# A block-recurrent attention with an activated two-layer product: 69 elementwise steps moved to GpSimd, fewer filler products, new orders

## The chip, the core and the metric

The kernel runs on one core of a Trainium2 chip. A core has five engines with a queue each: TensorE (PE, matrix products from SBUF into PSUM), VectorE (DVE), ScalarE (ACT, activations and copies), GpSimd (POOL) and SyncE (SP, which issues transfers). ACT and POOL can issue transfers as well. Each engine works off its own instructions in the order in which they were written, and waits on semaphores for the others. The metric is the device time of one execution in microseconds. Times are medians of a few runs; the profile is of one more execution.

## The reference

All data are float32. Attention part, with `x` of 8 x 8 x 512 x 64 and `state` of 8 x 8 x 32 x 64:

```python
scores = scale * x @ state^T ;  a = softmax(scores) ;  xread = a @ state
scores2 = scale * state @ x^T ; a2 = softmax(scores2) ; sread = a2 @ x
attn = concatenate([xread, sread], axis=2)          # 8 x 8 x 544 x 64
```

Then, on the 4352 rows of 512 that this gives:

```python
h = rows @ w_in                                     # 512 -> 2048
g = h * erf(softplus(h))
out = g @ w_out                                     # 2048 -> 512
```

## The kernel before

**Tiling.** A batch `b` (eight of them) has 512 token rows and 32 state rows. Batch 0 is computed plainly while the weights arrive. For the others the hidden width is cut in two halves `u`: a first phase does batches 1 to 7 with half 0 (`unit(b, 0, ...)`), then the state rows of all batches are done, then a second phase does batches 1 to 7 and 0 with half 1. The products use a scheme with seven block products instead of eight (`seven`, `second_product`), in the second phase and for the last two batches of the first one twice over (`twice_product`). Such a scheme trades matmuls for sums of blocks. Those sums are much of VectorE's work:

- `mixed` (L838 to L854): the state of a batch times a half of `w_in`, evicted by ACT into `m`, and four sums of 128x512 (L849).
- `sums_y` (L875): four sums of 128x256 of the transposed attention weights, per batch.
- `first_product` (L937): seven products give `h` through PSUM; ACT copies (L949), DVE adds (L951, L955), ACT takes Softplus (L959).
- `serf` (L974, L977): Erf on ACT, then the product with `h` on DVE; `sums_a` (L988): four sums of 128x1024 on DVE.
- `twice_product` (L1239 sums of the left factor, L1257 products, L1267 copies, L1272 adds). `total` (L1182) adds two results before they are stored. `put` stores over POOL's queue with an add into memory (L1177) or over SP's queue (L1174). In the last batch `join_others` reads back what is stored, adds the rest (`join`, L1189) and stores (`store`, L1193); the last stores are at L1306.

**Conversion of the weights.** The weights arrive as 64-bit numbers in `raw`. `convert` makes float32 of them in five steps: ACT scales the upper words (L558) and the lower words (L560), DVE shifts (L562), adds the lower part (L564) and puts the sign in (L566). The first eight pieces are converted in the prologue; for the second half of the weights, `stage` fetches and converts sixteen smaller pieces during the first phase.

**The prologue.** `begin0` computes batch 0's scores, softmax and transposes. Between its steps PE runs filler products (`spare_products`, which calls `warm`, L115): products of the identity with itself, whose results nobody reads. Each is two records of 128x128.

**The order of the work.** Nothing is issued where it stands in the code. Every step is entered by `op(engine, cost, at, go, reads, writes, ...)`, which notes on which earlier steps it depends. `ORDER` holds for each engine a list written out by hand in which order its steps stand in its queue. `emit` walks these lists with the given costs to find a common order of starts, and writes the instructions in it. The costs decide nothing on an engine: there the list alone counts. `either` (L152 to L175) puts a copy on DVE if its name is in the set `BY_VECTOR`, and on ACT otherwise.

**What is where.** GpSimd computes nothing but the identity at the start; its queue holds transfers: the fetches of the second half of the weights (L543, L549), stores of converted weights and the accumulating stores (L1177).

Of the kernel before, what the change touches and what calls it, by code (L numbers as in the profile page):

```python
# [9 lines left out]
F32 = mybir.dt.float32  # L10
# [7 lines left out]
def kernel(  # L18
# [121 lines left out]
    def op(engine, cost, at, go, reads=(), writes=(), table=None, land=0.0, pipe=0.0):  # L140
# [14 lines left out]
        x1 st s01 ta0 ta1 z1 m020 m021 u0 u1 m120 m121 sn11 sn40 sn41 sn51 sn70""".split())  # L155

    def either(name, cost, out, in_, at, reads, writes, by=None):

        def vector():
            if by:  # L160
                nc.vector.tensor_scalar(out(), in_(), by(), None, op0=ALU.mult)
            else:
                nc.vector.tensor_copy(out(), in_())

        def scalar():
            if by:
                nc.scalar.activation(out=out(), in_=in_(), func=ACTF.Copy, scale=by())
            else:
                nc.scalar.copy(out(), in_())

        if name in BY_VECTOR:
            op(DVE, cost[1], at, vector, reads, writes)
        else:
            op(ACT, cost[0], at, scalar, reads, writes)
# [3 lines left out]
            0 5 1-2 8 3 6 4 9 15 7 10 12 22 13 16-18 25 19-20 11 23-24 14 26 28 27 29-30 21 32 31  # L178
            33-34 70 54 69 53 61 45-46 62 55 35 64 36-37 47 38 72 40 39 50 41 58 57 71 73 63 49 43
            52 42 48 60 56 44 77-78 59 79 51 76 82 81 83 80 66 84-85 93 86-87 75 68 89 74 88 90 65  # L180
            67 92 91 102 106 94 97 107 103-104 108 105 109 118 95 110-111 114-115 112 96 113 116
            98-99 117 130 119 122 132-133 123 131 134 124-125 137 135 120 136 140 139 138 141 121
            142-143 100 144 126 101 127-129 145 147 149-151 177 153-154 179-180 155 178 181 184 165
            182 166 152 167 183 161 187 168 156 186 185 188 157-158 189 159 190 162-164 191 146 160
            148 169-170 192 194 171-172 224 196-197 173-174 198-199 226 225 227 175 200 176 228 231
            201-202 212 203 229 208 230 204-205 233 206 234 232 209 235 210 213 236 211 237 207 214
            216 238 193 217-219 195 215 241 239 220-221 243-245 271 246 222 273 240 223 274 247
            251-252 272 275 242 255 276 248 278 256 277 249 281 257 280 279 250 259 282 253 260 284
            283 254 258 285-286 261 263-265 288 287 266 318 262 290 321 291 267 322 292 319 289 268
            323 293 269-270 320 298 294 325 295 324 296 299 327-328 302 300 303 329 301 304 326 305  # L190
            330 297 331 310-312 306 313 307-309 333 332 334 364 314-315 336 366 316 365 367 317 337
            339 368 343 338 371 344 369 345 370 347 335 373 340 374 341-342 346 375 372 349 406 376
            348 350 377 357 407 351 408 359 358 353 360 352 361 354 410 355 363 362 356 385 409 387
            386 388 378 389 411 390-391 379-382 412-413 383 399 384 414-415 392 401 416 418-419 417
            394 434 393 435 395-396 403 438 400 402 404 440 397 441 436 398 405 437 442-443 439
            444-446 432 422-423 447 428 424-425 449 448 430 433 464 420-421 429 426 467 466 427 431
            468 465 471 469-470 450 474 473 472 475 451 462 476-477 454-455 452-453 479 478 456
            458-459 508 457 460 463 461 511 509 487 510 480 489 488 512 515 481 490 513 491 483 482
            492 518 484 514 519 493 517 516 520 501 485-486 521 494 522-523 495-496 502 552 503-504
            497-498 553 505 555 554 506-507 556 499 531 500 532-533 524 558 535 557 534 559 536-537  # L200
            526 525 560 528 562 545 561 563 529 527 564-565 530 547 567 566 549 546 538 548 596 540
            539 598 541-542 599 551 600 603 550 543 575 544 576-578 597 579 568 602 601 580 569-570
            606 572 604 607 605 581 571 608-609 573 610-611 574 589 640 590-592 582 642 593 643 583
            594 644 647 595 584 619 641 586 585 620 645 587-588 621 646 612 650 613 615 614 623 622
            648 651 616 624 652 618 617 653 626 649 625 655 654 628 627 633 630 684 629 634 636 687
            685-686 635 688 637 689 638 632 690 639 691 631 693 663 694 656 664 695 692 665 657 659
            667 666 658 697 668 696 660 699 698 669 661 728 677 662 678-679 731 670 729-730 681 672
            680 671 674 673 675-676 682 732 700 683 701 733 707 734 709 708 735 711 702 710 703-704
            712 738 736 706 705 737 739 714 713 740-741 721 715 722-723 716-717 725 742-743 726 718
            724 719 772 727 774-775 720 773 751 776 744 777 746 779 752 745 753 747 782 781 778 755  # L210
            754 783 748 780 784 756-757 749 785 765 750 766 758 768 767 759-762 769 763-764 770 786
            771 787-790 793 791 795 794 792 797 800 796 801-802 798-799 804 803 807 805-806 808-809
            814 810-811 816 815 812 817-818 813 819-820""",
        ACT: """
            0-3 5 10 4 11-12 6-7 13 8-9 30 29 14 31 15-17 52 32 53 19 18 33-37 20-21 38 22-23 39-40
            25 24 41-43 28 26-27 45 48 44 47 46 50 54-55 49 51 56 61 64 63 62 65 57-58 67 66 68 70
            69 71-72 92 91 73-74 83 101 76 102 84-85 75 77 60 86 79-80 78 81-82 87-89 131 90 99 132
            59 96 100 143 97 93 103-104 94-95 98 133 135 134 145 136 144 147 107 149 106 108 148 138
            105 139 150 137 146 151 156 153 158 157 155 159 154 162 160-161 152 141 140 163-165 142
            169-170 166-167 176 175 113 172 168 171 185-187 111 188 178-179 181 189 194 109-110 112  # L220
            196 177 114 191 197-198 193 195 192 190 199-200 208 183 174 173 207 201 180 202-203 182
            210-211 184 204 117 209 205 212 120 221 119 206 223 115 222 118 224 214 116 217 215 225
            230-232 213 235 233 226 228 234 236 219 227 237 218 123 229 238 124 243 239 244 220 216
            240-241 126 249 121 125 248 245-246 242 122 258 247 130 259 129 254 260-261 251 250 262
            267 252-253 265 269-270 268 263 266 264 127 271-274 128 280 255-256 283 282 275 281 276
            286 277 285 287 284 296 278 257 298-299 279 292 300 297 289 288 305 290 306 302 307 310
            301 291 303 308-309 294 311 304 312-316 295 317 321 318 320 319 344 293 345 322 324 346
            329 347-348 330 325 353 351 332 327 323 349 326 355 331 354 328 350 358 356 359 334 352
            357 360 333 339 361-362 340 363-365 335 386 341 336 342 337 343 371 338 372 374 373
            366-367 369 368 375 370 387-388 381 389 376 390-391 382 377-378 392 399 393 384 394-396  # L230
            379 397-398 383 385 380 401-402 405 407 403 406 400 415 414 412-413 404 408-409 417
            410-411 418-419 422 420 423 421 426 428 427 429 425 432 424 431 430 433-437 440 439 441
            416 442 463 438 465 448 443 464 466 449 451 467 472 444 452 474 445-446 450 475 471 458
            468 473 447 469 476 470 479 477 453 478 485 487 480 488 481-482 454 486 483 459 484 509
            461 511 460 456 455 512 457 462 494-495 510 489 496-497 513 498 514 490 517-518 492 520
            519 521 504 491 523-524 522 516 515 525-526 505 527-528 533 507 531 493 499 534 532 555
            529 500 506 501 530 556-557 502 508 540-541 503 558 543 535 544 559 564 542 536 566 563
            567 561-562 565 538 570 537 568 560 571 539 572 579 578 577 580 550 569 601 551 573-574
            545 553 603 552 602 575-576 554 586 546 604 548 547 605 610 587 549 581 607 582 612 589
# [589 lines left out]
    def mixed(b, u, at):  # L829
# [17 lines left out]
        def sub(o, x, y, how=ALU.subtract):  # L847
            v = views_x()
            tt(v[o - 1], v[x - 1], v[y - 1], op=how)  # L849
# [20 lines left out]
    def sums_y(b, at):  # L870
        y_of = Y_of(b)

        def sub(o, x, y):
            v = views_a(b)
            tt(v[o - 1], v[x - 1], v[y - 1], op=ALU.subtract)  # L875
# [839 lines left out]
```

## Time and profile before

| | us |
|---|---|
| median of 3 runs | 698.82 (698.72 to 699.63) |
| the profiled execution | 699.4 |
| its span, first to last instruction | 697.6 |
| PE busy | 690.2 (99%) |
| DVE busy | 586.3 (84%) |
| ACT busy | 467.3 (67%) |
| POOL busy | 85.9 (12%) |
| PE's last matmul ends | 693.15 |
| dense products start (L614) | 20.71 |

The clock granted to TensorE is 1.00 over the run. HBM traffic averages 132 GB/s. A line of the groups shows the code line, the engine, the operation, output<-input, shapes and count, then busy time, the mean of one in ns, the idle time of the engine before them and what ended it. `PEq`, `SPq` and `POOLq` are what an engine's sequencer does by itself. Matmul ends in the trace are modelled, so PE's stalls are better read from the view of waits than from its busy time.

### The profile page before, as it was taken

The page shows a single profiled execution, that of the slowest core. Times are in us where ns is not written, and L with a number is a line of the kernel's source. Part 1 is how long each engine was busy: PE and PEld are TensorE (multiplying, and loading weights), DVE is VectorE, ACT ScalarE, POOL GpSimd, SP SyncE. Part 2 cuts the span into 40 slices and gives each one's busy share as a digit, 9 for nine tenths or more (in the row PEclk, how much of TensorE's full clock was granted, in tenths as well). Part 3 has the DMA queues.
Part 4 walks back from the last instruction along what each step waited for, and adds up shares of the span by engine and source line. Part 5 has one row for each costly group of instructions (what it writes and reads, how often), then busy time and mean ns, then how long its engine had stood idle before and what let it go on. Part 6 is the DMA issues. An engine that isn't in the chain of part 4 may idle for free.

```text
span 697.6 us, 13137 instructions
## 1 busy us (share of the span) xinstructions
PE 690.2 (99%) x5193; PEld 583.9 (84%) x5193; DVE 586.3 (84%) x900; ACT 467.3 (67%) x847; POOL 85.9 (12%) x93
## 2 busy tenths in 40 slices
PE   9999999999999999999999999999999999999997
PEld 8534678787878888899998879898989898998996
DVE  5999899998989999988945679696959696869797
ACT  5987988869596766756263774858485748385832
POOL 0000110102010010000200200002322133022332
PEclk9999999999999999999999999999999999999999
DMA  8858878867968854140729311213736158026495
GB/s 263 231 144 170 216 177 212 221 143 238 239 210 180 230 166 181 62 167 1 160 83 346 47 54 46 69 16 80 95 73 87 55 65 155 1 31 92 64 148 106
DMA packets 133741, 92.87 MB, mean 133 GB/s; under 512 B 93744, under 2 KB 120752, under 8 KB 133168
## 3 DMA queue, kind: packets, MB, share of 16 engines
q1 hardware_dynamic: 114336, 61.88, 32.0%
q0 software_dynamic: 18800, 29.63, 22.5%
q8 instruction: 41, 0.67, 0.4%
q10 hardware_dynamic: 544, 0.52, 0.2%
q14 instruction: 20, 0.16, 0.1%
HBM read 50.86 MB, written 41.16 MB: 132 GB/s over the span
## 4 chain that ended last, share of the span: by engine, by line
PE 89%; DVE 4%; ACT 1%; issue 0%; DVEq 0%
PE o L1257 29%; PE h L937 19%; PE o L1021 18%; PE at L937 7%; PE o L1440 4%; PE o L639 2%; PE h L1391 2%; PE at L838 2%; PE h L838 2%; PE at L799 1%; PE h L706 1%; PE at L1391 1%; DVE ring L977 1%; PE at L614 1%; DVE ring L988 0%
## 5 line engine op out<-in xcount | busy, mean ns | idle before, releaser
L949 ACT COPY ring<-h 128x512 f32<-128x512 f32 x120 | 69.8, 586 | 70.2 <-PE h L937 63.8
L977 DVE TENSOR_TENSOR ring<-ring 128x1024 f32<-128x1024 f32 (+1 forms) x64 | 73.3, 1153 | 23.9 <-ACT ring L974 23.9
L937 PE MATMUL h<-aT,m 128*128 128x256 f32 x360 | 91.6, 381 | 0.2 <-ACT m L844 0.2
L1021 PE MATMUL o<-w_out,ring 128*128 128x256 f32 x320 | 77.7, 382 | 0.0
L959 ACT ACTIVATE ring<-ring 128x512 f32<-128x512 f32 x120 | 72.5, 634 | 6.5 <-PE o L1257 3.7
L937 PEld LDWEIGHTS h<-aT,m 128*128 128x128 f32 x360 | 65.5, 190 | 10.1 <-issue 1.3
L988 DVE TENSOR_TENSOR ring<-ring 128x1024 f32<-128x1024 f32 x60 | 72.8, 1218 | 0.4
L1021 PEld LDWEIGHTS o<-w_out,ring 128*128 128x128 f32 x320 | 59.6, 190 | 11.9 <-DVE m L566 1.7
L1257 PE MATMUL o<-w_out,w_in 128*128 128x128 f32 x512 | 69.1, 276 | 0.3 <-DVE ring L1282 0.3
L1257 PEld LDWEIGHTS o<-w_out,w_in 128*128 128x128 f32 x512 | 64.7, 192 | 2.8 <-issue 0.8
L1257 PE MATMUL o<-w_out,ring 128*128 128x128 f32 x480 | 64.8, 276 | 0.1
L974 ACT ACTIVATE ring<-ring 128x1024 f32<-128x1024 f32 (+1 forms) x64 | 62.4, 1005 | 0.2
L1257 PEld LDWEIGHTS o<-w_out,ring 128*128 128x128 f32 x480 | 60.4, 192 | 1.8 <-DVE ot L1272 0.3
L1021 PE MATMUL o<-raw,ring 128*128 128x256 f32 x240 | 59.8, 380 | 0.0
L1021 PEld LDWEIGHTS o<-raw,ring 128*128 128x128 f32 x240 | 45.2, 190 | 8.6 <-issue 2.5
L1257 PE MATMUL o<-raw,ring 128*128 128x128 f32 x360 | 49.6, 276 | 0.1
L1257 PEld LDWEIGHTS o<-raw,ring 128*128 128x128 f32 x360 | 46.1, 192 | 2.1 <-ACT ring L974 0.8
L1177 POOL DMA_DIRECT2D out_dram<-oo x16 | 25.9, 1736 | 164.5 <-DVE m L1239 77.8
L1257 PE MATMUL o<-raw,xT 128*128 128x128 f32 x320 | 41.8, 277 | 0.0
L1257 PEld LDWEIGHTS o<-raw,xT 128*128 128x128 f32 x320 | 38.6, 192 | 2.4 <-ACT ring L959 0.8
L1177 POOL DMA_DIRECT2D out_dram<-m x15 | 22.1, 1624 | 104.9 <-ACT ring L959 38.2
L937 PE MATMUL h<-sy,sx 128*128 128x256 f32 x120 | 31.2, 382 | 0.0
(269 smaller groups left out, 1400.5 us busy)
## 6 DMA issues: line engine op xcount, KB each, us to landing
x<-in_x_dram SPq DMA_DIRECT2D x30, 256.0 KB, 4.7
xq<-in_x_dram SPq DMA_DIRECT2D x112, 64.0 KB, 2.5
out_dram<-oo SPq DMA_DIRECT2D x10, 512.0 KB, 3.6
raw<-in_moe_w_in_dram SPq DMA_DIRECT2D x8, 512.0 KB, 6.6
raw<-in_moe_w_out_dram SPq DMA_DIRECT2D x4, 1024.0 KB, 7.4
kept_a<-aT SPq DMA_DIRECT2D x8, 512.0 KB, 4.8
raw<-in_moe_w_out_dram POOLq DMA_DIRECT2D x8, 512.0 KB, 5.7
raw<-in_moe_w_in_dram POOLq DMA_DIRECT2D x8, 512.0 KB, 5.7
```

The source lines that it names most:

```text
L838: nc.tensor.matmul(out=bank(names[k])[Ns * p:Ns * p + Ns, :], lhsT=st[r, b, q], rhs=of_group[2 * u + j][r, :, i, :], start=True, stop=True)
L937: nc.tensor.matmul(out=out_[:, i], lhsT=x_[:, q:q + P], rhs=y_, start=(start and i == 0), stop=(i == 1), skip_group_check=not start)
L949: op(ACT, 0.5, t, lambda: nc.scalar.copy(out_(), view(bank(name))), [name], w)
L959: op(ACT, 0.53, t, lambda: nc.scalar.activation(out=part(splane, k), in_=part(hplane, k), func=ACTF.Softplus), area(hplane, ks=[k], os=[o] ...
L974: op(ACT, 0.085 + 0.875 * share, at + n, lambda s_=s_: nc.scalar.activation(out=s_, in_=s_, func=ACTF.Erf), [], area(splane, ks=[k], os=os ...
L977: op(DVE, 0.065 + 1.075 * share, at + n + 1, lambda s_=s_, h_=h_: tt(s_, s_, h_, op=ALU.mult), area(hplane, ks=[k], os=os), area(splane, k ...
L988: op(DVE, 1.14, at + k, lambda k=k, x_=x_, y_=y_, how=how: tt(get("h", k), get(*x_), get(*y_), op=how), area(v[x_[0]], ks=[x_[1]]) + area( ...
L1021: nc.tensor.matmul(out=view(name)[:, h], lhsT=lhs[:, i, :], rhs=weight_of[n]()[:, u, i, :], start=(start and h == 0 and i == 0), stop=(h = ...
L1177: op(GP, 1.2, t, lambda: nc.gpsimd.dma_start(out=quad(r, c), in_=one(v), accum_op=ALU.add), every(*v), [("out", b, r, c)], land=3.0, pipe=2.0)
L1257: nc.tensor.matmul(out=out_[:, Q2 * k:Q2 * k + Q2], lhsT=lhs[:, k, i], rhs=rhs[:, i], start=first, stop=(k == len(ns) - 1 and i == 1), ski ...
L1391: nc.tensor.matmul(out=bank(bk)[:, P * i:P * i + P], lhsT=x_[:, i, k], rhs=y_[:, k], start=(start and i == 0 and k == 0), stop=(i == GF - ...
L1440: nc.tensor.matmul(out=bank("o%d" % bk)[:, E2 * c:E2 * c + E2], lhsT=ring[:, w_[w], plane, k][:, i, :], rhs=weight_of[n]()[:, u, i, :], st ...
```

## The change

1. **Steps on GpSimd.** `either` gets an argument `run`, and now also enters five kinds of steps that were fixed on one engine: the upper scaling of `convert` (names with `*`; ACT, or GpSimd), the add of `convert` (names with `+`), the sums of `mixed` (`x...`), `sums_y` (`y...`), `total` (`t...`) and `join` (`j...`). For these, a name that is in `BY_VECTOR` stays where it was, and one that is not goes to GpSimd. By the new set 69 steps go there: 10 upper scalings, 14 conversion adds, 19 sums of `mixed`, 15 of `sums_y`, 10 of `total` and one of `join`.
2. **Copies between DVE and ACT.** Of the copies that were free to go to either before, some change sides: the first state copy `st`, the attention copies `ta0` and `ta1` and four copies of the reads go from DVE to ACT; some others go the other way.
3. **Stores at the end.** `store` and the last stores are split over the queues of SP and ACT.
4. **Fillers.** 31 instead of 45 filler products.
5. **Orders.** All five lists are new. The order in ACT's list loads the activation table 58 times instead of 51. PE's list now begins with a filler on the identity.

```diff
     BY_VECTOR = set("""
-        x1 st s01 ta0 ta1 z1 m020 m021 u0 u1 m120 m121 sn11 sn40 sn41 sn51 sn70""".split())
-
-    def either(name, cost, out, in_, at, reads, writes, by=None):
+        x2 s00 +i00 *i01 *i1 +i1 *o0 +o0 *i2 +i2 +i3 *o2 +o3 z1 m011 m020 m021 u0 u1 m120 m121 y06
...
+        t712100 t713021 t712121 t712030 j0000 j0001 t012100 j0121 j0120 t013021 j1130 j1120 j1030""".split())
+
+    def either(name, cost, out, in_, at, reads, writes, by=None, run=None):
...
         if name in BY_VECTOR:
-            op(DVE, cost[1], at, vector, reads, writes)
+            if name[0] == "*":
+                op(ACT, cost[1], at, lambda: run(None), reads, writes)
+            else:
+                op(DVE, cost[1], at, (lambda: run(nc.vector)) if run else vector, reads, writes)
+        elif run:
+            op(GP, cost[0], at, lambda: run(nc.gpsimd), reads, writes)
         else:
             op(ACT, cost[0], at, scalar, reads, writes)
...
-        spare_products("at0", 2, 9.2)
+        spare_products("at0", 1, 9.2)
...
-            spare_products("o%d" % g, 2 if g else 6, 12.6 + 5 * g)
+            spare_products("o%d" % g, 2, 12.6 + 5 * g)
...
-           [("out0", 1)] * late, RAW(k, [h]), land=3.0 * late, pipe=2.0 if late else 1.7)
+           [("out0", 1)] * late, RAW(k, [h]), land=3.0 if late else 0.0 if f else 2.9,
+           pipe=2.0 if late else 1.7)
...
-        op(ACT, 1.05 if full else 0.57, at, lambda: nc.scalar.activation(
-            out=to, in_=hi.bitcast(F32), func=ACTF.Copy, scale=2.0 ** -112), reads, writes)
+        def upper(on):
+            if on:
+                on.tensor_scalar(to, hi.bitcast(F32), 2.0 ** -112, None, op0=ALU.mult)
+            else:
+                nc.scalar.activation(out=to, in_=hi.bitcast(F32), func=ACTF.Copy,
+                                     scale=2.0 ** -112)
+
+        either("*" + named, (1.73, 1.05) if full else (0.96, 0.57), None, None, at, reads, writes,
+               run=upper)
...
-        op(DVE, 1.15 if full else 0.6, at + 1, lambda: tt(d, d, lo, op=ALU.add),
-           reads + [("lo", key)], writes)
+        either("+" + named, (2.4, 1.15) if full else (1.3, 0.6), None, None, at + 1, reads + [("lo", key)],
+               writes, run=lambda on: on.tensor_tensor(d, d, lo, op=ALU.add))
...
-            op(DVE, 0.6, at + 3, lambda o=o, x=x, y=y, how=how: sub(o, x, y, how),
-               [X_of[x - 1], X_of[y - 1]], [X_of[o - 1]])
+            either("x%d%d%d" % (b, u, o), (1.3, 0.6), None, None, at + 3,
+                   [X_of[x - 1], X_of[y - 1]], [X_of[o - 1]],
+                   run=lambda on, o=o, x=x, y=y, how=how: sub(on, o, x, y, how))
...
-            op(DVE, 0.335, at, lambda o=o, x=x, y=y: sub(o, x, y),
-               [y_of[x - 1], y_of[y - 1]], [y_of[o - 1]])
+            either("y%d%d" % (b, o), (0.75, 0.335), None, None, at,
+                   [y_of[x - 1], y_of[y - 1]], [y_of[o - 1]],
+                   run=lambda on, o=o, x=x, y=y: sub(on, o, x, y))
...
-            op(DVE, 0.6, t, lambda: tt(one(to), one(vx), one(vy), op=ALU.add),
-               every(*vx) + every(*vy), every(*to))
+            either("t%d%d%d%d%d%d" % (b, u, *to, *vx), (1.3, 0.6), None, None, t,
+                   every(*vx) + every(*vy), every(*to),
+                   run=lambda on: on.tensor_tensor(one(to), one(vx), one(vy), op=ALU.add))
...
-                op(DVE, 0.6, t, lambda: tt(mine(r, c), mine(r, c), one(v), op=ALU.add),
-                   every(*v), own(r, c))
+                either("j%d%d%d%d" % (r, c, *v),
+                       (1.3, 0.6), None, None, t, every(*v), own(r, c),
+                       run=lambda on: on.tensor_tensor(mine(r, c), mine(r, c), one(v), op=ALU.add))
...
-                op(SP, 0.4, t, lambda: nc.sync.dma_start(out=quad(r, c), in_=mine(r, c)),
+                e, on = (ACT, nc.scalar) if r else (SP, nc.sync)
+                op(e, 0.5, t, lambda: on.dma_start(out=quad(r, c), in_=mine(r, c)),
                    own(r, c), [("out", b, r, c)], pipe=0.8)
...
-                op(SP, 0.4, at + 26, lambda h=h, cols=cols: nc.sync.dma_start(
+                e, on = (SP, nc.sync) if h or qs.start else (ACT, nc.scalar)
+                op(e, 0.55, at + 26, lambda h=h, cols=cols, on=on: on.dma_start(
                     out=quad(0, 1)[:, h, cols], in_=mine(0, 1)[:, h, cols]),
...
-    for k, at in enumerate((12.7, 13.4, 14.1, 15.3, 16.5, 17.3, 18.5, 20.6)):
-        spare_products("o%d" % (2 + k // 5), 3, at)
+    for k, at in enumerate((12.7, 13.4, 14.1, 15.3, 16.5)):
+        spare_products("o%d" % (2 + k // 3), 3, at)
```

Where `either` is called with `run`, its first cost is GpSimd's and its second that of the engine before. The five lists of `ORDER` are replaced as a whole and are not shown.

More of the change, by code (lines that the diff above doesn't have):

```diff
@@ L183 @@
[L183 to L203, printed above, removed]
@@ L298 @@
+            30 35 9 33 59 58 60 44 39 36 34 40 42 38 45 61-62 41 46-47 43 50 64-66 52 48 63 67 54 51
+            55 49 69 68 53 70 72-74 71 75-79 82 80-81 83-84 92-94 88 86 85 87 103 89-90 95-96 98 100
+            104 91 106 110 97 114 105 107-108 99 101-102 113 111 109 124-125 112 116 115 120 118-119
+            117 121 123 122 135 126 136 129-130 127 133 131 138 144 137 128 140 139 132 134 143 142
+            146 141 145 147-152""",
     }
```

217 lines of the change are left out of this document (122 added, 95 removed), and 4 rows, old and new, of the table ORDER.

## The prediction

> **What bounds the kernel now.** I read the busy shares first, then what TensorE (PE) waited for, then the busy time by stage, then the order of time at both ends.
>
> ```profile
> PE 690.2 (99%) x5193; PEld 583.9 (84%) x5193; DVE 586.3 (84%) x900; ACT 467.3 (67%) x847; POOL 85.9 (12%) x93
> ```
>
> PE is busy for 690.2 of 697.6 us. A busy PE may hide waiting, so the view of waits decides, here for PE alone:
>
> ```profile
> PE o L115 <- PEq L1699: 0.8, 1, 0.8
> PE o L446 <- ACT xT L169: 0.5, 1, 0.5
> PE o L1257 <- DVE ring L1282: 0.3, 1, 0.3
> PE o L456 <- DVE ring L481: 0.3, 1, 0.3
> PE at L614 <- DVE m L163: 0.3, 1, 0.3
> PE o L1257 <- DVE ot L1272: 0.3, 1, 0.3
> PE h L937 <- ACT m L844: 0.2, 1, 0.2
> ```
>
> That is 2.7 us in all, 1.6 of it in the first 20 us. PE has no real waiting left in the long middle, so lighter VectorE (DVE) or ScalarE (ACT) work can bring next to nothing there. What can be won is at the two ends; what can be lost is everywhere. The stages (columns: length, busy time of PE, weight loads, DVE, ACT, POOL, clock, DMA):
>
> ```profile
> 66.00:206.00 140.00, 140.00 (x988) 109.61 (x987) 131.50 (x178) 112.57 (x192) 14.66 (x24) 1.00 0.76 204
> 206.00:346.00 140.00, 139.75 (x1069) 121.47 (x1068) 129.52 (x198) 87.31 (x160) 8.10 (x11) 1.00 0.52 143
> 380.00:520.00 140.00, 140.00 (x1011) 123.27 (x1010) 105.31 (x178) 94.73 (x178) 17.07 (x16) 1.00 0.30 63
> ```
>
> The reader is to see that DVE is 93% busy while the first weight half is used (66 to 346 us) and 75% afterwards: a delay on DVE has 19 us of idle time to vanish in before 346 us, and plenty later. The start and the end, in order of time:
>
> ```profile
> 15.65 0.68 DVE L491 TENSOR_REDUCE m2b<-ring 128x1 f32<-128x512 f32 x1
> ...
> 19.27 0.69 DVE L481 TENSOR_TENSOR ring<-ring,z1b 128x512 f32<-128x512 f32 x1
> ...
> 20.71 3.67 PE L614 MATMUL h<-aT,m 128*128 128x512 f32 x8
> ...
> 692.21 1.61 SPq L1193 DMA_DIRECT2D out_dram<-ring  x2
> ...
> 693.87 1.09 SPq L1306 DMA_DIRECT2D out_dram<-ring  x2
> ```
>
> PE's dense work begins at 20.71, released by a chain of DVE steps; at the end the last two stores stand behind two others in SyncE's (SP) queue.
>
> **Step 1, fillers.** Filler products go from 45 to 31. Each is two records of 112 ns, so 14 x 0.224 = 3.1 us of PE time leaves, all before 26 us. They fill time in which PE would wait, so alone they give nothing; they count as far as the chain under them becomes shorter.
>
> **Step 2, the chain before 20.71.** Ahead of the second L481 (19.27 to 19.96) leave DVE's queue: two L491 (0.6 us each as issued), one L564 (0.72, to GpSimd), one L493 (0.11), together 2.0 us. Against it, the copy of xT now stands ahead of the first maximum and the first evictions share ACT with the copy of the state, which I put at 0.5 by their starts (the maximum at 9.4 instead of 8.91). The attention copies L163 go to ACT, where the like takes 0.58 instead of 0.68. L614 then starts at about 19.2 instead of 20.71: -1.5 us. Bounds: -3.1 (all fillers become time won) and +0.6, because PE's first instruction is now a filler on the identity, which POOL finishes only at 1.31, while PE began at 0.78. I take -1.5, the count.
>
> **Step 3, the end.** The four stores that SP issues ahead of its last two (the last of them 692.21 to 693.82) become one; the others go to ACT's queue, idle by then. The next could go when its sum is done at about 693.5 instead of 693.87: -0.4 us. The last join goes to GpSimd, ready at 692.45, some 1.2 instead of 0.69 us, then ACT's issue; it ends beside SP's last one. Bounds -0.5 and +0.5.
>
> **Step 4, the 69 steps on GpSimd (POOL).** They are 10 scalings (3 of 128x1024, 7 of 128x512) from ACT, and from DVE 14 conversion adds (2 of 1024), 19 sums of L849, 15 of L875, 10 of L1182, one join of L1189. By rows DVE loses 42 x 0.685 + 15 x 0.417 + 2 x 1.226 = 37.5 us. ACT loses 3 x 1.13 + 7 x 0.68 = 8.2 us but has 58 table loads instead of 51, 7 x 1.28 = 9.0 us; only 5 of the 58 wait for anything, so they run in ACT's idle time (70.2 us before L949 alone) and I cost them at nothing. If that cover were gone, they would delay evictions by 1.28 us each.
>
> No row shows GpSimd doing such a step. Its nearest rows:
>
> ```profile
> masks.py:199 POOL TENSOR_SCALAR_AFFINE_SELECT ident<-ident 128x128 f32<-128x128 f32 x1 | 0.3, 287 | 0.1
> L1699 POOL MEMSET const-float32-1.0<- 128x1 f32 x1 | 0.1, 98 | 0.0
> ```
>
> 287 less 98 over 127 elements is 1.49 ns an element: an estimate of 0.86 us for a scaling of 512, 1.6 for 1024. For two inputs the ends are DVE's 0.68 and twice the slope, 1.6 (512); I take the middle, 1.15 (0.63 for 256, 2.15 for 1024). GpSimd's new work is then 42 x 1.15 + 15 x 0.63 + 2 x 2.15 + 7 x 0.86 + 3 x 1.6 = 73 us, 43 of it before the second weights are stored (L1104, 256 us before). It has room: POOL is 12% busy. By the order, 30 matmuls of first_product wait directly for POOL, 39 instructions of DVE and 34 of ACT too.
>
> The unknown is whether GpSimd and DVE disturb each other at SBUF. Rows hint that they may: a DVE step with one input runs 128x1024 in 0.68 us (L562), one with two takes 1.22 (L988), so two inputs use up what one input has twice. The low end is nothing. For the high end, every GpSimd step holds up a DVE step with two SBUF inputs. Such steps (L977 34.4, L988 34.1, L849 19.1, L875 11.3, L564 and L566 21.7, L734 and L751 14.6, and smaller) fill about 57% of 66 to 346 us, so DVE is held for 0.57 x 43 = 25 us before that point and 0.57 x 30 = 17 us after, as much as it was relieved of (37.5). DVE would be as full as before, but in lumps of a microsecond, on orders made for a lighter DVE. After it the idle quarter of DVE takes that. Ahead of it I let a quarter through to PE: 25 / 4 = 6.2 us; half, 12.4, is the upper end and 0 the lower. I take 6.2, between ends that no row decides.
>
> The Trainium skill, "SBUF — State Buffer", section "Who interferes with whom", says that a VectorE instruction with two SBUF inputs and a GpSimd instruction that reads SBUF exclude one another for a whole instruction. By that rule the holding of DVE is real; without it the sum would be that of the first rival. No run here shows it yet: POOL's rows of before read no tile.
>
> **The sum.** The profiled execution took 699.4 us, 697.6 of span and 1.8 around it, 0.6 above the median. 699.4 - 1.5 - 0.4 + 6.2 = 703.7; as a median 703.1.
>
> **The queues passed.** On POOL the sums stand among the accumulating stores, 1.2 to 3.2 us each; on SP the state and xq loads are reordered, issue to landing 2.5 to 5.8 us, needed tens of microseconds later: nothing. The changed landing figure for the first loads only informs the order.
>
> **Rivals.**
> 1. GpSimd disturbs nobody. Then steps 1 to 3 remain, and of the waits in the middle (0.3 to 0.5 us each) perhaps 0.5 go: 699.4 - 1.5 - 0.4 - 0.5 - 0.6 = 696.4, faster. For it: POOL is idle and DVE gets 37.5 us lighter. Place: 66 to 346 us. It decides if less than 1.9 us of GpSimd's delays reach PE. Chance 0.30.
> 2. Both effects cancel, 1.5 to 3.5 us through: 698.9. Chance 0.12.
> 3. The POOL queue is late: a sum of L849 stands behind a store that itself waits (POOL waited 44.6 us once for ACT's L844), and PE waits for the sum. Against it: POOL's mean load stays low. One sum late by one store, 1.7 us, in six of the fifteen units is 10 us: 699.4 - 1.9 + 10 - 0.6 = 706.9. Chance 0.12.
> The forecast, DVE held up and a quarter through, has 0.46.
>
> **How the numbers follow.** Slower by over 0.2% (1.4 us, about what a measurement of this kernel can tell from none): 0.46 + 0.12 = 0.58, less 0.01 for a weak form, 0.57. Faster 0.30. Within 0.2%: 0.13. The range reaches from rival 1 (696.0) to the upper end of step 4 with a little less than 12.4 us through (709.0). The likeliest case by itself spans 700.5 to 709.
>
> **What would show it.** Step 2: L614's successor starts at about 19.2 and PE's first instruction after 1.3. Step 3: no issue of SP stands between 692.2 and the sums of the end, and the span ends sooner than 4.4 us after PE's last matmul (693.15 of 697.6 before). Step 4: POOL shows some 73 us more; DVE's two-input groups (L977, L988 and their successors) have a mean above 1.22 us, or DVE starts late with nothing it waits for; PE's waits in 66 to 346 us grow from under 1 us to several. I am wrong if those means stay at 1.22 and PE's waits stay below 3 us.

## The result, and the profile after

The changed kernel takes 707.16 us (median of 4 runs, 706.54 to 708.15) where the kernel before took 699.01 on the same chip (698.72 to 699.63): a ratio of 1.0117, with a 95% interval of 1.0099 to 1.0134. It is 8 us slower. Its profiled execution took 708.15, with a span of 706.1 and a granted clock of 1.00, as before.

The busy shares of the changed kernel, from the page:

```profile
PE 690.2 (98%) x5165; PEld 581.6 (82%) x5165; DVE 580.5 (82%) x837; ACT 472.6 (67%) x848; POOL 190.2 (27%) x162
```

DVE issues 63 instructions fewer and is only 5.8 us less busy; 37.5 had been taken off it. POOL has 104.3 us more. What PE waited for, in the same form as before (total, times, longest):

```profile
PE o L1284 <- DVE ot L1299: 1.9, 2, 1.5
PE at L115 <- POOL ident masks.py:199: 1.4, 1, 1.4
PE h L961 <- DVE aT L777: 1.3, 2, 0.7
PE o L1045 <- DVE ring L1001: 1.1, 1, 1.1
PE o L728 <- DVE xq L719: 1.0, 1, 1.0
PE at L618 <- DVE w_in L588: 0.9, 1, 0.9
PE o L468 <- DVE ring L493: 0.8, 2, 0.5
PE o L1284 <- DVE w_in L1266: 0.7, 1, 0.7
```

With the six smaller lines left out here, these are 11.7 us against 2.7 before, 9.7 of them behind DVE. No line but that of the identity names POOL: PE doesn't wait for GpSimd's results itself, but for a DVE that runs late. DVE waits for GpSimd's results for 3.8 us in all; what that costs is tried below. The stages (length, then busy time of PE, weight loads, DVE, ACT and POOL, clock, DMA):

```profile
66.00:206.00 140.00, 135.85 (x952) 105.86 (x951) 131.04 (x165) 110.40 (x183) 45.67 (x45) 1.00 0.85 212
206.00:346.00 140.00, 140.00 (x1060) 120.74 (x1059) 123.06 (x174) 94.57 (x165) 24.28 (x24) 1.00 0.49 148
380.00:520.00 140.00, 138.93 (x984) 122.70 (x983) 104.60 (x170) 89.89 (x170) 28.28 (x21) 1.00 0.31 66
520.00:660.00 140.00, 137.45 (x1081) 124.84 (x1080) 110.55 (x155) 90.48 (x180) 57.07 (x44) 1.00 0.52 80
```

The last of these stages before:

```profile
520.00:660.00 140.00, 139.97 (x1084) 128.86 (x1084) 111.21 (x174) 92.70 (x186) 35.32 (x30) 1.00 0.46 68
```

PE loses 4 us in the first of these stages and another 2.5 in the last (139.97 before), where DVE has 29 us of idle time. DVE has 13 instructions fewer than before in the first stage (165 instead of 178) and the same busy time, so the ones that are left have become longer. The groups by form show it (busy time, mean of one in ns, idle time before); the first two lines are of the kernel before:

```profile
L988 DVE TENSOR_TENSOR ring<-ring 128x1024 f32<-128x1024 f32 x60 | 72.8, 1218 | 0.4
L977 DVE TENSOR_TENSOR ring<-ring 128x1024 f32<-128x1024 f32 x56 | 68.0, 1220 | 23.9 <-ACT ring L974 23.9
...
L1012 DVE TENSOR_TENSOR ring<-ring 128x1024 f32<-128x1024 f32 x60 | 75.5, 1267 | 0.4
L1001 DVE TENSOR_TENSOR ring<-ring 128x1024 f32<-128x1024 f32 x56 | 72.7, 1309 | 31.4 <-ACT ring L998 31.4
...
L871 POOL TENSOR_TENSOR sx<-m,sx 128x512 f32<-128x512 f32 x8 | 13.2, 1647 | 53.9 <-PE o L1284 25.9 <-DVE sx L871 25.5 <-ACT h L931 2.5
L587 POOL TENSOR_TENSOR w_out<-w_out,raw 128x512 uint32<-128x512 uint32 x7 | 12.2, 1743 | 25.6 <-issue 15.7 <-DVE w_out L584 6.8 <-ACT raw L582 3.0
L575 POOL TENSOR_SCALAR w_out<-raw 128x1024 f32<-128x1024 f32 x2 | 5.7, 2866 | 8.2 <-DMA raw<-in_moe_w_out_dram 8.2
L1216 POOL TENSOR_TENSOR ring<-ring,ot 128x512 f32<-128x512 f32 x1 | 1.3, 1261 | 4.2 <-DVE ot L1299 4.2
```

L1012 and L1001 are the sums and the product of `sums_a` and `serf` (L988 and L977 before). GpSimd's additions of 128x512 take from 1.26 us to over 1.7, its scaling of 128x1024 takes 2.87. The 21 groups of its new steps add up to 107.0 us. The two ends, in order of time:

```profile
19.52 0.66 PE L468 MATMUL o<-ident,ring 128*128 128x128 f32 x4 [0.49 <-DVE ring L493]
20.01 2.82 PE L636 MATMUL h<-aT,m 128*128 128x512 f32 x6
23.71 0.67 PE L618 MATMUL at<-w_in,ring 64*32 64x256 f32 x16 [0.88 <-DVE w_in L588]
...
701.74 0.71 PE L1284 MATMUL o<-w_out,w_in 128*128 128x128 f32 x4
702.16 0.99 SPq L1334 DMA_DIRECT2D out_dram<-ring  x2
```

The dense work starts at 20.01 instead of 20.71, but stops for 0.88 us behind a conversion step. PE's last matmul ends at 702.45, 9.3 us later than before, and the span ends 3.65 us after it instead of 4.5.

### The profile page after: what moved, and what is told of

The parts are those of the page before. It is cut to its first block, busy times and chain, and to the rows that moved or that the text cites. A ratio compares the mean times of both kernels' runs of the same rounds, so it can differ in the third digit from the quotient of the medians.

```text
span 706.1 us, 13177 instructions
## 1 busy us (share of the span) xinstructions
PE 690.2 (98%) x5165; PEld 581.6 (82%) x5165; DVE 580.5 (82%) x837; ACT 472.6 (67%) x848; POOL 190.2 (27%) x162
## 4 chain that ended last, share of the span: by engine, by line
PE 69%; DVE 14%; ACT 4%; issue 3%; POOL 1%; DMA 1%; DVEq 0%; ACTq 0%; POOLq 0%
PE o L1284 28%; PE h L961 14%; PE o L1045 12%; PE at L961 6%; PE h L1419 3%; DVE ring L1001 2%; PE o L1468 2%; DVE ring L1012 2%; PE h L860 1%; PE at L860 1%; PE at L1419 1%; ACT ring L983 1%; DMA out_dram<-m 1%; PE at L821 1%; ACT ring L998 1%
## 5 line engine op out<-in xcount | busy, mean ns | idle before, releaser
L1001 DVE TENSOR_TENSOR ring<-ring 128x1024 f32<-128x1024 f32 (+1 forms) x64 | 77.8, 1231 | 32.4 <-ACT ring L998 32.3
L1012 DVE TENSOR_TENSOR ring<-ring 128x1024 f32<-128x1024 f32 x60 | 75.5, 1267 | 0.4
L961 PEld LDWEIGHTS h<-aT,m 128*128 128x128 f32 x360 | 65.4, 190 | 10.9 <-issue 3.4
L1201 POOL DMA_DIRECT2D out_dram<-oo x16 | 22.5, 1434 | 99.9 <-DMA out_dram<-oo 43.8
L961 PE MATMUL at<-sy,sx 128*128 128x256 f32 x120 | 31.0, 381 | 0.7 <-DVE ring L979 0.6
L1266 DVE TENSOR_TENSOR w_in<-ring 128x512 f32<-128x512 f32 (+1 forms) x50 | 30.0, 610 | 2.0 <-PE o L1284 1.6
```

The source lines that it names most:

```text
L961: nc.tensor.matmul(out=out_[:, i], lhsT=x_[:, q:q + P], rhs=y_, start=(start and i == 0), stop=(i == 1), skip_group_check=not start)
L1001: op(DVE, 0.065 + 1.075 * share, at + n + 1, lambda s_=s_, h_=h_: tt(s_, s_, h_, op=ALU.mult), area(hplane, ks=[k], os=os), area(splane, k ...
L1012: op(DVE, 1.14, at + k, lambda k=k, x_=x_, y_=y_, how=how: tt(get("h", k), get(*x_), get(*y_), op=how), area(v[x_[0]], ks=[x_[1]]) + area( ...
L1201: op(GP, 1.2, t, lambda: nc.gpsimd.dma_start(out=quad(r, c), in_=one(v), accum_op=ALU.add), every(*v), [("out", b, r, c)], land=3.0, pipe=2.0)
L1266: factor=factor: tt(flat(factor(o)), flat(factor(x_)), flat(factor(y_)), op=how),
```

## The experiments

The theory is the prediction's: GpSimd and VectorE hold each other at SBUF, that is, a step of the one lasts longer because the other reads there at the same time ("the hold" below), and the lengthened DVE steps reach PE. The rivals: the new orders are worse by themselves; results come late from GpSimd or its queue, without any hold.

**The hold by itself.** A kernel of twelve stretches, in each of which DVE and POOL run a row of steps on tiles of their own:

```diff
+    for v, n, g, m in ((None, 0, pool_two, 8), (two_sbuf, 8, None, 0), (two_sbuf, 12, pool_two, 8),
+                       (half_sbuf, 16, pool_two, 8), (one_psum, 16, pool_two, 8), ...
+        for k in range(max(n, m)):
+            if k < m:
+                g(k)
+            if k < n:
+                v(k)
+        meet()
```

> This kernel computes nothing of the reference and writes zeros; it measures the disputed cost by itself. In twelve stretches GpSimd and VectorE each run a row of like steps, alone and then side by side on tiles of their own that the other never touches, so that no step waits for data of the other engine. The theory that the two hold each other at SBUF expects: a VectorE addition of two SBUF tiles of 128x1024, alone about 1.22 us, rises to 1.5 us or more in the mean beside GpSimd's additions, one of 128x512 from 0.68 to about 1.0; a GpSimd addition of 128x512, some 1.26 us alone, becomes longer beside them; an addition with one input in PSUM (0.68), a maximum and a transpose (1.2 each) stay as they are; GpSimd's memset, which reads nothing, leaves VectorE at 1.22. The rival that GpSimd disturbs nobody expects the same means in every pair of stretches, within 3%. The rival that GpSimd is simply slow expects its addition of 128x512 to take 1.6 us or more even when it is alone.

The groups of that kernel, each taken from the part of one stretch in which both were at work (the first two lines: each alone); the third number is the mean in ns:

```profile
L71 POOL TENSOR_TENSOR go<-ga,gb 128x512 f32<-128x512 f32 x8 | 9.8, 1260 | 8.0 <-DVE go L43 8.0
...
L53 DVE TENSOR_TENSOR do<-da,db 128x1024 f32<-128x1024 f32 x7 | 8.0, 1219 | 0.0
...
L53 DVE TENSOR_TENSOR do<-da,db 128x1024 f32<-128x1024 f32 x7 | 15.5, 2277 | 0.0
L71 POOL TENSOR_TENSOR go<-ga,gb 128x512 f32<-128x512 f32 x7 | 15.4, 2238 | 0.0
...
L56 DVE TENSOR_TENSOR do<-da,db 128x512 f32<-128x512 f32 x7 | 11.7, 1744 | 0.0
...
L62 DVE TENSOR_SCALAR do<-da 128x1024 f32<-128x1024 f32 x7 | 11.7, 1745 | 0.0
...
L71 POOL TENSOR_TENSOR go<-ga,gb 128x512 f32<-128x512 f32 x7 | 8.6, 1263 | 0.0
L59 DVE TENSOR_TENSOR do<-da,pp 128x512 f32<-128x512 f32 x14 | 8.5, 681 | 0.0
...
L65 DVE TENSOR_REDUCE red<-da 128x1 f32<-128x1024 f32 x8 | 9.1, 1211 | 0.0
...
L68 DVE STREAM_TRANSPOSE do<-da 128x1024 f32<-128x1024 f32 x8 | 9.1, 1206 | 0.0
...
L53 DVE TENSOR_TENSOR do<-da,db 128x1024 f32<-128x1024 f32 x7 | 8.0, 1218 | 0.0
L77 POOL MEMSET go<- 128x1024 f32 x8 | 7.2, 953 | 0.0
```

The two engines work in turns: a DVE addition of 1.22 and a GpSimd addition of 1.26 both become 2.28 and 2.24. Everything that the theory named as free is free: a step with an operand in PSUM (0.68), a maximum, a transpose, and everything beside GpSimd's memset. Not expected was the DVE scaling with one input: alone it took 0.68 in the same stretch, beside GpSimd 1.75. The Trainium skill, "SBUF — State Buffer", section "Who interferes with whom", names both cases, two SBUF inputs and the fast one-input forms, and calls the shared access an exclusive lock; its section "SBUF: two separate sides" says that the engine that comes second waits for the whole instruction of the first. The trace agrees on which steps are held; the turns of 2.28 are 0.2 us shorter than the two durations together (2.48).

**Giving the steps back, and idle reads.** The 69 steps return to DVE and ACT, each at its place in the order of the changed kernel; then GpSimd in addition reads the identity, into a tile that nobody uses, once each of these steps is done.

```diff
-            op(GP, cost[0], at, lambda: run(nc.gpsimd), reads, writes)
+            op(GP, cost[0], at, lambda: run(None if name[0] == "*" else nc.vector), reads, writes)
```
```diff
+            def back(n=1024 if cost[0] > 1.5 else 256 if cost[0] == 0.75 else 512):
+                run(None if name[0] == "*" else nc.vector)
+                ...
+                    nc.gpsimd.tensor_tensor(spare[:, 0:m].rearrange("p (r n) -> p r n", n=P),
+                                            wide_id[:, 0:m // P], wide_id[:, 0:m // P], op=ALU.add)
+                    tc.add_manual_dep(...)      # waits for the step
+            op(GP, cost[0], at, back, reads, writes)
```

> The changed kernel with its 69 steps given back to VectorE and ScalarE at the same places in the written orders; the fillers, the first loads, the last stores and all other orders stay as changed. The main theory (holding at SBUF costs the time) expects the gain of the two ends without the loss in the middle: about 697 us, some 2 us under the kernel before and 10 under the changed one, and TensorE's waits back from 11.7 to 4 us or less. The rival that the new orders themselves cost the time expects 704 us or more, since VectorE then also has the 37 us of steps back that these orders no longer allow for. The rival that GpSimd's results come late, without any holding, expects about 697 too; the next kernel parts those two.

> The kernel of the run before, in which in addition GpSimd adds the identity to itself into a spare tile that nobody reads, 72 times in all (57 of 128x512, 15 of 128x256), each as soon as the step that GpSimd did in the changed kernel is done on its own engine. No result of GpSimd is used, so none can come late, but it reads SBUF about as much as in the changed kernel. The theory of holding expects a loss against the run before of about the 9 us that the changed kernel loses by TensorE's end, or more, since VectorE now also carries the steps: 704 to 712 us, and a mean of the two-input groups of VectorE above 1.25. The rival of late results expects no loss: within 1 us of the run before, 696 to 698. If the new orders alone are the cause, this run and the one before lie together at 704 or more.

Given back: 704.9 us, ratio 1.0087 (1.0072 to 1.0103). That was expected by the rival of the orders, not by the main theory. With idle reads: 715.83, ratio 1.0236 (1.0219 to 1.0254), so reads whose results nobody uses cost 10.9 us more, above the 704 to 712 that were expected. Both are true, then: the new orders lose 6 us when DVE does the steps itself, and reading by GpSimd loses 11 in them. The mean of L1012's group is 1.218 with the steps given back and 1.241 with the idle reads, under the 1.25 that was expected; but DVE as a whole is busy for 607.9 us instead of 585.1.

**Idle writes; old orders with GpSimd; the ends alone.** The idle reads are replaced by fills of a spare tile. Next, the kernel before with its own orders, in which only the 69 steps are handed to GpSimd. Last, the kernel before with 31 fillers and two queues for the last stores.

```diff
-                    nc.gpsimd.tensor_tensor(spare..., wide_id..., wide_id..., op=ALU.add)
+                    nc.gpsimd.memset(spare, 0.0)          # 2 to 8 times a step
```
```diff
+    def shared(name, engine, cost, at, run, reads, writes):
+        own = None if engine == ACT else nc.vector
+        op(engine, cost, at, lambda: run(own if name in OWN else nc.gpsimd), reads, writes)
```
```diff
-        spare_products("at0", 2, 9.2)
+        spare_products("at0", 1, 9.2)
...
-                op(SP, 0.4, t, lambda: nc.sync.dma_start(out=quad(r, c), in_=mine(r, c)),
+                on = nc.scalar if r else nc.sync
+                op(SP, 0.4, t, lambda: on.dma_start(out=quad(r, c), in_=mine(r, c)),
```

> The kernel with the 69 steps back on VectorE and ScalarE (704.9) in which GpSimd, at the same places as in the run with the idle reads and with the same waits, only fills a spare tile of 128x256 with zeros, two to eight times a step, about 65 us in all by the fill of 128x1024 that took 0.95. Holding at SBUF by GpSimd's reads expects no loss, since the memset left VectorE's additions at 1.22 us: 704 to 706. The rival that any work on GpSimd (its queue in front of the stores, its semaphores) costs the time expects most of the 10.9 us of the idle reads again: 711 or more.

> The kernel before, with all its own orders, fillers and stores, in which only the 69 steps go to GpSimd, each at the place that it had in the order of VectorE or ScalarE. With the three others (old orders without GpSimd 699.1, new orders without 704.9, new orders with 707.2) this completes a table of two by two. If the new orders fit the work on GpSimd, as orders searched for that purpose should, old orders with GpSimd are worse than new ones with it: 709 to 716, by the loss of 10.9 that the idle reads brought less what VectorE is relieved of. If GpSimd's work and the new orders are two separate costs that add, this run shows 699.1 + 2.3 = 701.4. If GpSimd's steps are harmless and the orders are the whole loss, it stays at 699 or falls below.

> The kernel before with two parts of the change alone: 31 filler products instead of 45, and the last stores over two queues; all steps stay on their engines and in their old orders. The stores: the span ended 4.5 us after TensorE's last product before and 3.65 after, so 0.8 us is expected from them. The fillers: the dense work began 0.7 us sooner in the changed kernel, where the order of the first steps was changed too; with the old order of those steps between 0 and 0.7. Together 697.6 to 698.4, which is 0.7 to 1.5 under before. The rival that these parts cost something by themselves (a clock that falls without fillers, stores that collide) expects 699.5 or more.

Idle writes: 705.27, ratio 1.0094 (1.0079 to 1.0109), 0.4 over the kernel without them, with POOL 171.5 us busy as in the run with the idle reads (173.2). GpSimd's work as such is nearly free; its reads are not. Old orders with GpSimd: 715.71, ratio 1.0257 (1.0227 to 1.0287). The two costs do not add to 701.4: in the old orders GpSimd costs 16.8 us, in the new ones it costs 2.3 against the steps given back. The new orders fit that division of the work better. The four executions with the old orders differ with the granted clock: 713.93 and 714.75 at 0.999, 716.66 at 0.997, 719.37 at 0.992. The groups of `sums_a` and `serf` have means of 1.298 and 1.291 us there.

The ends alone: 699.45 (ten runs), ratio 1.0007 (0.9998 to 1.0017): nothing, where 0.7 to 1.5 was expected. The trace of the profiled execution shows why for the start. The last two lines are of the kernel before:

```profile
19.29 0.66 PE L456 MATMUL o<-ident,ring 128*128 128x128 f32 x4 [1.16 <-DVE ring L481]
19.98 3.67 PE L614 MATMUL h<-aT,m 128*128 128x512 f32 x8
...
40.45 1.17 ACT L560 ACTIVATE raw<-raw 128x1024 uint32<-128x1024 uint32 x1 [1.13 <-DMA raw<-in_moe_w_out_dram]
47.46 0.69 DVE L630 TENSOR_TENSOR ring<-ring,h 128x512 f32<-128x512 f32 x1 [0.75 <-ACT ring L626]
...
39.79 1.17 ACT L560 ACTIVATE raw<-raw 128x1024 uint32<-128x1024 uint32 x1
47.37 0.65 DVE L630 TENSOR_TENSOR ring<-ring,h 128x512 f32<-128x512 f32 x1
```

The dense work begins at 19.98, 0.7 sooner; but the first matmul of `first_product`, at 66 us, starts only 0.1 sooner. What ends the head start is the weights. The piece that L560 converts was asked for 0.7 us sooner than before (at 32.17 instead of 32.90) and landed 0.7 later (40.43 instead of 39.77). ACT waits for pieces of weights for 3.0 us between 20.7 and 66 us, where it waited for 0.9; DVE, 0.7 us ahead until then, waits 0.75 for ACT and is no longer ahead. Why the pieces landed later stays open. At the end the span closes 4.3 us after the last matmul instead of 4.5, yet the ten executions last 2.13 us longer than their spans in the mean, those of the kernel before 1.77.

**Orders searched anew.** Two kernels whose five orders were searched with a plan that knows the hold, one with the steps on GpSimd and one with the steps given back.

```diff
         PE: """
-            8 0-1 5 2-3 6 4 9 7 15 17 12 18 16 10 20 13 22 19 11 21 14 23-25 27 26 30 29 28 31 42 66
+            0-1 5 2-3 8 4 6-7 9 12 20 17 13 15 10 16 18 11 22 21 19 29 27 14 23-25 28 26 30-31 66 43
...
```

> The changed kernel with the same 69 steps on GpSimd and the same parts; only the five written orders are new. They were searched again with a plan that knows what the first run measured: a GpSimd step and a VectorE step with SBUF inputs alone never run at the same time (reductions, transposes and steps with a PSUM input are free to), a scaling of 128x1024 on GpSimd takes 2.77 us and not 1.73. If holding is the whole of what the changed kernel loses in its middle, orders that reckon with it get most of the 8 us back: 699 to 702, with TensorE's waits back under 6 us. If the loss lies elsewhere (queue of the stores, results handed from engine to engine), orders made around the hold change little: 705 to 709.

> The changed kernel with the 69 steps back on VectorE and ScalarE, fillers and last stores as changed, and the orders searched again in the same way for this division of the work (704.9 with the orders of the changed kernel). The theory that those orders were only right for a VectorE relieved of the steps expects the kernel before again, less what the end brings: 698 to 700. The rival that one of the other parts (31 fillers, copies moved between VectorE and ScalarE, two queues at the end) costs the 6 us expects 703 or more.

Both missed by far: 721.55 with GpSimd, ratio 1.0321 (1.0304 to 1.0339), and 714.32 without, ratio 1.0219 (1.0204 to 1.0234). The second has no hold at all and is still 9.4 us worse than the same division of work in the orders of the changed kernel. The searched orders are thus bad by themselves, for a reason that these runs don't show, and the pair says nothing on the question. PE is busy for 697.1 and 693.5 us in them, with the same 5165 matmuls that take 689.1 with the steps given back.

**GpSimd without its reads.** This parts the hold from all else: each of the 69 steps stays on GpSimd, at its place, with its waits and its readers, but leaves out the sum or the scaling: it copies one column of each operand and then fills the result's tile twice. Once in the changed kernel, once in the kernel before with its old orders.

```diff
+    class Fill:
+        def tensor_tensor(out, x, y, op=None):
+            for t in (x, y):
+                nc.gpsimd.tensor_copy(first(out), first(t))
+            for _ in range(2):
+                nc.gpsimd.memset(out, 0.0 if out.dtype == F32 else 0)
...
-            op(GP, cost[0], at, lambda: run(nc.gpsimd), reads, writes)
+            op(GP, cost[0], at, lambda: run(Fill), reads, writes)
```

> The changed kernel with its own orders, in which each of the 69 steps stays on GpSimd with the same waits, the same readers and about the same time (one column of each operand is copied, then the result's tile is filled with zeros twice), but reads hardly anything: 0.38 + 2 x 0.48 us for 128x512 by the copies and fills measured alone. It leaves out the sums and conversions themselves, so its output is not the reference's. VectorE stays relieved of the steps, the results still come from GpSimd, and GpSimd's queue is as full. If holding at SBUF is what the changed kernel pays, this one is the prediction's first rival made real: 695.5 to 698, and the means of the two-input groups back at 1.22. If results that come late from GpSimd, the queue, or the new orders are what costs, it stays at 703 or more; if both, it ends in between, and its distance to 707.2 is the part of the hold.

> The same with the orders, fillers and stores of the kernel before: the 69 steps stand on GpSimd at their old places, filled with zeros in place of sums and conversions (left out, as in the run before). The kernel with the real steps took 715.7. If the hold is the whole of those 16.8 us, this run ends at 697 to 701. If results come late there, since a GpSimd step takes longer and its place in GpSimd's queue is behind stores, it stays above 707.

New orders: 699.79 (ten runs), ratio 1.0009 (1.0000 to 1.0019); that is far from the 703 or more of the rivals, but over the 695.5 to 698 that were expected. Old orders: 700.28, ratio 1.0011 (1.0001 to 1.0021). The page, the stages and the groups of the first:

```profile
PE 687.5 (99%) x5165; PEld 582.0 (84%) x5165; DVE 554.7 (80%) x837; ACT 472.8 (68%) x848; POOL 206.0 (30%) x369
```
```profile
66.00:206.00 140.00, 138.41 (x991) 108.03 (x992) 124.82 (x165) 113.23 (x188) 55.27 (x129) 1.00 0.86 217
...
520.00:660.00 140.00, 139.63 (x1081) 128.98 (x1080) 103.97 (x163) 94.18 (x188) 61.84 (x85) 1.00 0.51 75
```
```profile
L1024 DVE TENSOR_TENSOR ring<-ring 128x1024 f32<-128x1024 f32 x60 | 72.6, 1217 | 0.4
L1013 DVE TENSOR_TENSOR ring<-ring 128x1024 f32<-128x1024 f32 x56 | 67.6, 1219 | 34.0 <-ACT ring L1010 34.0
```

POOL is even busier than in the changed kernel (206.0 against 190.2), and the same 837 DVE instructions take 554.7 us instead of 580.5: the hold adds 25.8 us to DVE. L1012 and L1001 (here L1024 and L1013) are back at 1.22. The fills don't deliver sooner than the real steps did: their own durations add up to 130.1 us, those of the real steps to 107.0.

The hold falls on few steps. Both kernels issue the same 837 DVE instructions in the same order; compared one by one, 33 are longer by more than 0.1 us in the changed kernel, by 27 us together. One case, from the stage in which DVE is idle for 29 us (the last line is of the filled kernel):

```profile
551.26 2.93 POOL L1208 TENSOR_TENSOR m<-sc,m 128x512 f32<-128x512 f32 x1
551.62 3.13 DVE L1266 TENSOR_TENSOR xT<-ring 128x512 f32<-128x512 f32 x2
555.94 0.49 PE L1284 MATMUL o<-w_out,ring 128*128 128x128 f32 x2 [1.51 <-DVE ot L1299]
...
544.13 1.29 DVE L1278 TENSOR_TENSOR xT<-ring 128x512 f32<-128x512 f32 x2
```

Beside one addition on GpSimd two DVE sums take 3.13 us instead of 1.29, and PE waits 1.51 for what stands behind them in DVE's queue. The six kernels side by side, in us:

| who does the 69 steps | orders before | orders changed |
|---|---|---|
| DVE and ACT | 698.9 (kernel before) | 704.9 |
| GpSimd | 715.7 | 707.2 (changed kernel) |
| GpSimd, filling instead of reading | 700.3 | 699.8 |

Reading down, the hold is worth 15.4 us in the old orders (13.3 between the two profiled executions, whose clocks are alike) and 7.4 in the new ones. Waits on GpSimd's results and its queue, with all the rest of the change, are left with 0.6 us over the 699.15 of the same session. The middle cell on the right is the changed kernel: its orders take back half of what GpSimd's reads cost, and no kernel of the table is faster than the one before.

That the new orders need a light DVE is seen in their column: the steps given back cost 5.1 us against the filled ones, with the same fillers and stores. In the kernel with the steps given back, DVE has done 52.6 us of work by 66 us where the kernel before has done 57.3, and is then 95% busy to 206 us, while PE falls from 140.0 to 135.85 busy in that stage. That this late start is the cause is argued from these numbers and was not tried by itself, and it can't be the whole: matmul by matmul, PE lags 4.0 us behind the filled run by 206 us, still 4.0 at 400, and 5.8 at the end. The changed kernel lies within 1 us of the one with the steps given back from 66 to 400 us, 0.2 behind it at 400, and loses the rest of its 2.3 us after that.

## Why the prediction was right or wrong

The direction and the range held, and the hold is real; the point, 703.1, was 4 us low. Against the kernel before I had booked -1.9 for the two ends and +6.2 for the hold. Measured are +0.6 for all that isn't hold (ratio 1.0009), and 7.4 for the hold. That 6.2 and 7.4 lie so close is luck: the place was half wrong, and the two factors behind the 6.2 were off in opposite ways (step 4).

- **Step 1**, fillers cost nothing and bring nothing alone: right. The 28 matmuls are gone (5165 instead of 5193; PE's busy time falls by 2.2 us with the ends alone) and the time is the same.
- **Step 2**, -1.5 from the shorter chain: this term failed twice. The start moved by 0.7 (20.71 to 20.01), within the bounds; and in the run with the ends alone what it moved was given back before 66 us. I asked when the dense work starts, and not what ACT, DVE and PE wait for after it: there the head start ran into weights that landed no sooner. PE's first instruction came at 1.36, as the step said.
- **Step 3**, -0.4 at the end: in the changed kernel the span does end 0.8 us sooner after the last matmul (3.65 instead of 4.5), twice what I said, but the kernels with two queues last longer outside their spans: 2.13 us in the mean of ten with the ends alone and 2.24 with the filled steps, against 1.77 and 1.78 of the kernel before beside them; the changed kernel's own four, 1.85. With only the fillers beside it, it brings nothing.
- **Step 4, the durations**: 73 us of new work for GpSimd was too little, it is 107.0. Its 1.15 for an addition of 128x512 was close to what it takes alone (1.26); the scaling of 128x1024 was far off (2.77 alone, I had 1.6). Much of the rest is GpSimd's own share of the hold: its additions of 128x512 have means from 1.26 to 2.1 us, since it waits for DVE as DVE waits for it.
- **Step 4, the hold**: right as a mechanism, and shown by the filled steps; wrong in where it reaches PE. Step by step against the filled run, DVE is held for 11.8 us before 346 us (I had 25) and for 13.4 after 400 (I had 17). PE's matmuls lag by 4.2 us at 346, by the same at 400, and by 9.3 at the end of the profiled execution. So a little over a third of the hold reached PE before 346 us, where I let a quarter through, and as much after 400, where I put it at nothing, because "the idle quarter of DVE takes that". It didn't: idle time of DVE in the mean does not cover a single step that comes late, as the case at 551 us shows. In the old orders this is plainer still: there the real steps put PE 0.4 us behind the filled ones by 400 us, where DVE is fullest, and 12.5 at the end. The 9.3 is of one pair of executions; between the medians it is 7.4.
- **Costed at nothing, rightly**: the extra table loads of ACT. ACT appears in PE's waits with 0.6 us in all, and the filled kernel, with the same loads, ends at +0.6.
- **Left out**: the orders. I gave them no price; they are worth 8.5 us with GpSimd (715.7 to 707.2) and cost 6 without.

The signs that step 4 named were seen: the means rose to 1.267 and 1.309, and PE's waits between 66 and 346 us to 4.0.

The rivals. The first, GpSimd disturbs nobody, was made real by the filled steps: 699.8, not 696.4, so even without a hold the change would not have won. The second, both effects cancel at 698.9, is out by the time itself. The third, a late POOL queue, is refuted as a main cause: with the queue as full, the waits the same and the results no sooner, 699.8 and 700.3.

## What to carry to other kernels

Before a step moves from VectorE to GpSimd, ask what it reads: beside VectorE steps with two SBUF inputs, an addition of 128x512 on GpSimd costs a VectorE step of 128x1024 beside it 1.06 us (2.28 instead of 1.22), more than the 0.68 that it takes on VectorE itself. What may stand beside it are reductions, transposes, steps with an operand in PSUM, and GpSimd work that only writes. Idle time of VectorE in the mean is no cover: what counts is whether a held step stands right before something that TensorE waits for. And where time is won at the start, follow it to the next waits of every engine, those for transfers too, before it is booked.

## What the runs showed of the hardware that was not expected

- VectorE's scaling of 128x1024 with one SBUF input is held by GpSimd as much as an addition of two: 0.68 us alone, 1.75 beside it.
- GpSimd's scaling, the slowest step that was moved, holds less than its addition. Beside a row of them (2.77 us alone, 3.14 here but for the first) ten VectorE additions took 2.05 and 1.21 in turns, so a whole addition ran within each scaling. With that form VectorE does not wait for the whole of GpSimd's instruction; the group:

```profile
L53 DVE TENSOR_TENSOR do<-da,db 128x1024 f32<-128x1024 f32 x10 | 15.5, 1622 | 0.0
L74 POOL TENSOR_SCALAR go<-ga 128x1024 f32<-128x1024 f32 x5 | 15.2, 3066 | 0.0
```

- The kernels with the last stores on two queues (and 31 fillers; the two were not parted) leave more time outside the span in some executions: 2.4 us or more in 12 of 44, never over 1.9 in those with one queue whose spans are on record.
